# Sparse attention and a multiplicative FFN on one core: batch 0 loaded first, a weight fold hosted behind FFN products, and both score groups in one phase

## The chip, the cores and the metric

The kernel runs on one core of one Trainium2 chip. The metric is the device time of one execution, in microseconds (us). A time is given as the median of several executions with their range. The span of a profile runs from the first to the last recorded instruction; it was about 1.7 us shorter than the device time. Executions of this kernel on one core are also marked fast or slow: slow is one that was over 1.5% above the fastest of the same kernel. Comparisons use the fast ones.

## The reference

Attention over 8 batches, 8 heads, 576 positions and 64 channels; half of the heads see the last 32 positions ("local"), half see every 32nd position ("strided"). Its output is the input of a feed-forward network (FFN) in which two projections are multiplied.

```python
rel = pos[:, None] - pos[None, :]
mask_local = (rel >= 0) & (rel < 32)                       # heads 0..3
mask_strided = (rel >= 0) & (pos[None] % 32 == pos[:, None] % 32)   # heads 4..7
attn = softmax(where(mask, q @ k.T / 8, -1e9))
x = (attn @ v).transpose(0, 2, 1, 3).reshape(4608, 512)
h = ((x @ w1) * (x @ w2)) @ w3                             # w1, w2: 512x1024; w3: 1024x1024
return h @ w_out                                           # w_out: 1024x512
```

No activation stands between `w3` and `w_out`, so the kernel computes their product once ("the fold", `w34 = w3 @ w_out`) and each FFN tile of 512 tokens needs only `x @ w1`, `x @ w2`, the product, and `@ w34`.

## The kernel before

Everything is cast to fp16 on load. A "pair" is two heads of one batch, so a batch has four pairs, two local and two strided. Five staging buffers (`stgp`) hold what has been loaded and not yet been cast. The attention of a pair is a list of phases; the function `host` interleaves phases with "units", the halves of FFN products, so that TensorE always has a product to do while the other engines work on the attention.

```python
def load_w3(pr):                    # 1 MB; staging buffer -> two w3n tiles (a pool of 2)
    st = stgp.tile([P, 2, DF], FP32, tag="stg"); nc.sync.dma_start(st, ...)
    ...                             # one cast on DVE, one on ACT
def load_local(b):                  # q, k: 96 partitions; casts on GpSimd, 0.87 us each
    ...
    st = stgp.tile([P, 4, LT, D], FP32, tag="stg")       # v with 32 earlier rows per block
    nc.sync.dma_start(st[:, :, 0, :], v[b, 0:4, 0:P]...)
    for h in range(4):
        nc.sync.dma_start(st[:, h, 1:LT, :], _ap(v[b, h], (LQ - 32) * D, ...))
    nc.gpsimd.tensor_copy(out=vt[:, :, :, 0:D], in_=st)
def load_strided(b): ...            # q, k, v: 72 partitions, casts on GpSimd

def ph_T(s, which):                 # transpose q or k of a pair, copy to SBUF
    ps = psM.tile([P, 1024], FP16, tag="m")              # psM: ONE buffer in PSUM
    ...
    if which == "q": nc.scalar.copy(out=o, in_=i)
    else:
        nc.vector.tensor_copy(out=o, in_=i)
        nc.gpsimd.memset(t[:, S:640], 0.0)
def ph_S(s, g):                     # scores of half a pair (64-row products), exp, mask
    ...
    nc.scalar.activation(out=pte[0:kr], in_=sps[0:kr, :, 0:288], func=AF.Exp, ...)
    nc.vector.tensor_mul(ptm[...], pte[...], <mask>)     # two inputs in SBUF
    nc.gpsimd.memset(ptm[:, 576:640], 0.0)
def ph_PV(s, g): ...                # probabilities x values, reciprocal, scaling
def ph_T2(s): ...                   # transpose the result into xT, through psM too

for p in range(np_):                # the order of the phases
    stream.append(lambda s=s: ph_S(s, 0))
    if p + 1 < np_: stream.append(lambda s=pairs[p + 1]: ph_T(s, "q"))
    stream.append(lambda s=s: ph_S(s, 1))
    if p >= 1: stream.append(lambda s=pairs[p - 1]: ph_T2(s))
    stream.append(lambda s=s: ph_PV(s, 0))
    if p + 1 < np_: stream.append(lambda s=pairs[p + 1]: ph_T(s, "k"))
    stream.append(lambda s=s: ph_PV(s, 1))

load_wo(); load_w3(0); load_w3(1)
... fold of blocks 0..3 ...         # 8 transposes and 8 products each
load_local(0); load_w3(2); load_w3(3); load_strided(0); load_w12()
host(later, 14)                     # fold of blocks 4..7 among batch 0's attention
load_local(1); att_only(batch_end[0]); load_strided(1)
for tch in range(NTILE):            # FFN tile tch, with the attention of batch tch + 1
    ...
```

The softmax here doesn't subtract the row's maximum and nothing guards it: scores larger than these inputs give would overflow.

## Time and profile before

| before | |
|---|---|
| time, median of 3 (range) | 312.8 us (312.19 to 313.06) |
| span of the profiled execution | 311.9 us |
| first FFN product starts | 65.4 us |
| a stage (one FFN tile and one batch of attention), tiles 1 to 5 | 28.71 us, within 0.02 |
| last stage (FFN tile alone) | 20.96 us |

A "stage" in this text is the distance between the first FFN products of two consecutive tiles, by the start times of the matmuls.

The page of the profile: busy time of two engines, and, in 40 slices of the span, the busy tenths of TensorE (PE), its granted clock and the share of the DMA engines.

```profile
span 311.9 us, 6533 instructions
...
PE 277.8 (89%) x2561; PEld 144.2 (46%) x2561; DVE 188.9 (61%) x361; ACT 134.6 (43%) x221; POOL 100.3 (32%) x192
...
PE   0285757689999999999999999999999999999994
...
PEclk9999897569999999999999999999999999999999
DMA  6999999998769989999895868660002001102003
```

PE is full from the ninth slice, near 66 us. Before it DMA is full. The table of stretches shows the same with numbers (busy us of each engine in the stretch, then granted clock, DMA share and GB/s):

```profile
core 0: us, PE busy (x) PEld busy (x) DVE busy (x) ACT busy (x) POOL busy (x), PEclk, DMA share, GB/s
8.00:16.00 8.00, 2.42 (x12) 1.34 (x13) 2.33 (x5) 2.68 (x3) 0.00 (x0) 1.00 1.05 363
40.00:48.00 8.00, 5.35 (x58) 3.14 (x58) 6.30 (x11) 4.18 (x8) 1.92 (x4) 0.97 1.05 364
...
56.00:64.00 8.00, 4.85 (x72) 3.96 (x72) 6.72 (x13) 2.69 (x5) 3.36 (x9) 0.50 0.92 191
64.00:72.00 8.00, 7.63 (x62) 3.93 (x60) 4.77 (x11) 3.97 (x7) 5.17 (x8) 0.75 0.96 201
100.00:140.00 40.00, 39.74 (x410) 20.80 (x409) 29.05 (x57) 20.83 (x35) 17.75 (x31) 1.00 0.97 209
```

From 8 to 72 us the DMA engines are busy all the time, and TensorE is not: 2.42 of 8 us at first, and 4.85 of 8 us at half clock just before the FFN starts. From 100 us on PE has 39.74 of 40 us. So two different limits hold, loads before about 65 us and TensorE after it.

Two further readings prepare the change. In the chain of work that ended last, the four products after a score phase (L224) take 0.97 us instead of 0.86:

```profile
77.12 0.86 PE bps L303 x4
77.98 0.24 PE sps L224 x8
78.22 0.97 PE aps L294 x4
79.19 0.26 PE ps L201 x8
```

The start times of the single products say where the 0.11 us comes from: leaving the 64-row score products costs about 95 ns (127 ns instead of 32), and ahead of them entering costs another 95 ns (310 ns instead of 215). The Trainium skill ("TensorEngine Tiling (Array Packing)", Key Properties) says that a change of the tiling mode drains TensorE; it gives no time for it. And in the stages from 123 to 267 us PE waited for almost nothing (waited-for instruction, us in total, times, longest):

```profile
engine line waited for: us in total, times, longest us
PE aps L294 <- ACT xT_112 L273: 1.3, 5, 0.3
```

### The profile page before, as it was taken

To read this page: it belongs to the slowest core of one execution; us is meant where nothing else is said; L and a number is where in the kernel's file an instruction comes from. 1 tells how busy PE (TensorE), PEld (TensorE's weight loads), DVE (VectorE), ACT (ScalarE), POOL (GpSimd) and SP (SyncE) were. 2 spreads that over 40 slices of the span, in tenths; PEclk is the share of its full clock that TensorE was granted. 3 is DMA by queue.
4 is the path that set the end of the run, shared out by engine and by line. 5 is a ranking of instruction groups with operands and counts; after the bars stand their busy time and mean duration, and the time that the engine had idled before them with its cause. 6 is when DMAs were issued, how large, how long until landed. Compare 5 with 4: busy or idle time off the path is not lost.

```text
span 311.9 us, 6533 instructions
## 1 busy us (share of the span) xinstructions
PE 277.8 (89%) x2561; PEld 144.2 (46%) x2561; DVE 188.9 (61%) x361; ACT 134.6 (43%) x221; POOL 100.3 (32%) x192
## 2 busy tenths in 40 slices
PE   0285757689999999999999999999999999999994
PEld 0133334554554554555455554555554555444441
DVE  1234378868767676777678566778765666442421
ACT  2323435345545544544454455445544543332330
POOL 5041520557463364435356171733230000000000
PEclk9999897569999999999999999999999999999999
DMA  6999999998769989999895868660002001102003
GB/s 227 371 228 324 229 376 232 177 210 150 183 165 261 196 189 248 226 182 206 243 223 113 217 191 159 143 187 36 0 36 101 2 3 74 62 0 101 35 2 136
DMA packets 48287, 50.23 MB, mean 161 GB/s; under 512 B 26496, under 2 KB 32640, under 8 KB 48256
## 3 DMA queue, kind: packets, MB, share of 16 engines
q1 hardware_dynamic: 48256, 49.82, 63.1%
q8 instruction: 20, 0.33, 0.5%
q14 instruction: 11, 0.09, 0.1%
HBM read 40.37 MB, written 9.44 MB: 160 GB/s over the span
## 4 chain that ended last, share of the span: by engine, by line
PE 83%; DVE 6%; ACT 5%; DMA 3%; issue 1%; SPq 0%; DVEq 0%; ACTq 0%
PE ops L317 26%; PE bps L303 20%; PE aps L294 20%; PE ps L201 5%; PE sps L224 5%; PE xps L250 4%; DMA st<-in_moe_w_dram 3%; PE ps L266 3%; ACT pte L229 2%; DVE w_115 L350 1%; ACT xT_112 L273 1%; DVE w3T_117 L346 1%; DVE xqs L258 1%; PE ps L344 1%; DVE t L212 1%
## 5 line engine op out<-in xcount | busy, mean ns | idle before, releaser
L297 ACT COPY asb<-aps 128x512 f32<-128x512 f32 x72 | 42.2, 586 | 68.8 <-PE aps L294 51.3
L229 ACT ACTIVATE pte<-sps 128x576 f16<-128x576 f32 (+1 forms) x64 | 41.6, 650 | 36.7 <-PE sps L224 36.1
L173 POOL CAST t<-st 72x1024 f16<-72x1024 f32 x32 | 33.0, 1059 | 25.0 <-DMA st<-in_q_dram 15.1
L258 DVE TENSOR_TENSOR xqs<-xps,rcp 96x384 f16<-96x384 f32 (+1 forms) x64 | 39.6, 619 | 2.1
L154 POOL CAST t<-st 96x768 f16<-96x768 f32 x32 | 26.9, 867 | 29.2 <-DMA st<-in_q_dram 17.1
L303 PEld LDWEIGHTS <-w2h 128*128 128x128 f16 x288 | 24.5, 98 | 22.1 <-issue 1.3
L294 PEld LDWEIGHTS <-w1h 128*128 128x128 f16 x288 | 24.6, 99 | 21.9 <-issue 0.6
L201 PEld LDWEIGHTS <-t 72*128 72x128 f16 (+1 forms) x448 | 25.1, 101 | 17.0 <-issue 4.0
L201 PE MATMUL ps<-id_79,t 72*128 72x72 f16 (+1 forms) x448 | 28.5, 206 | 3.1 <-ACT w3T_118 L347 2.8
L250 PEld LDWEIGHTS <-ptm 72*128 72x128 f16 (+1 forms) x448 | 23.2, 101 | 17.2 <-issue 2.2
L236 DVE TENSOR_TENSOR ptm<-pte,maskS 72x576 f16<-72x576 f16 x32 | 19.3, 603 | 17.7 <-ACT pte L229 17.5
L294 PE MATMUL aps<-xT_112,w1h 128*128 128x512 f16 x72 | 27.5, 382 | 1.6 <-ACT xT_112 L273 1.5
L232 DVE TENSOR_TENSOR ptm<-pte,maskL 128x576 f16<-128x576 f16 x32 | 18.4, 576 | 16.2 <-ACT pte L229 15.6
L294 PE MATMUL aps<-xT_109,w1h 128*128 128x512 f16 x72 | 27.8, 386 | 0.0
L303 PE MATMUL bps<-xT_109,w2h 128*128 128x512 f16 x72 | 27.6, 384 | 0.0
L294 PE MATMUL aps<-xT_111,w1h 128*128 128x512 f16 x72 | 27.5, 382 | 0.0
L294 PE MATMUL aps<-xT_110,w1h 128*128 128x512 f16 x72 | 27.5, 382 | 0.0
L303 PE MATMUL bps<-xT_110,w2h 128*128 128x512 f16 x72 | 27.3, 379 | 0.0
L303 PE MATMUL bps<-xT_112,w2h 128*128 128x512 f16 x72 | 27.3, 379 | 0.0
L303 PE MATMUL bps<-xT_111,w2h 128*128 128x512 f16 x72 | 27.2, 378 | 0.0
L329 ACT COPY osb<-ops 128x512 f32<-128x512 f32 x18 | 10.5, 586 | 33.0 <-PE ops L317 33.0
L224 PEld LDWEIGHTS <-t 64*128 64x128 f16 x448 | 11.1, 97 | 29.1 <-issue 22.5
(89 smaller groups left out, 415.0 us busy)
## 6 DMA issues: line engine op xcount, KB each, us to landing
st<-in_q_dram SPq DMA_DIRECT2D x16, 576.0 KB
st<-in_k_dram SPq DMA_DIRECT2D x16, 576.0 KB
out_dram<-osb SPq DMA_DIRECT2D x36, 256.0 KB
st<-in_moe_w_dram SPq DMA_DIRECT2D x8, 1024.0 KB
st<-in_v_dram SPq DMA_DIRECT2D x32, 160.0 KB
st<-in_v_dram SPq DMA_DIRECT2D x8, 576.0 KB
st<-in_moe_w_out_dram SPq DMA_DIRECT2D x2, 1024.0 KB
st<-in_v_dram SPq DMA_DIRECT2D x8, 128.0 KB
```

The source lines that it names most:

```text
L154: nc.gpsimd.tensor_copy(out=t[:, hp], in_=stv[:, 2 * hp:2 * hp + 2].rearrange("p h c d -> p c h d"))
L173: nc.gpsimd.tensor_copy(out=t[:, hp], in_=stv[:, 2 * hp:2 * hp + 2].rearrange("p h c d -> p c h d"))
L201: pe(nc.tensor.transpose(ps[:, c * w:(c + 1) * w], src[:, c].rearrange("p h d -> p (h d)"), id16[0:w, 0:w]))
L224: pe(nc.tensor.matmul(sps[:, h, i * w:(i + 1) * w], s.tT["k"][r, ks:ks + P], s.tT["q"][r, w * t:w * t + w], start=True, stop=True))
L229: nc.scalar.activation(out=pte[0:kr], in_=sps[0:kr, :, 0:288], func=AF.Exp, bias=0.0, scale=scale)
L236: nc.vector.tensor_mul(ptm[0:kr, 0:576].rearrange("p (a x) -> p a x", x=w), pte[0:kr].rearrange("p h (a x) -> p (h a) x", x=w), _ap(maskS, ...
L250: pe(nc.tensor.matmul(xps[:, h, i * 65:(i + 1) * 65], ptm[0:kr, c0:c0 + P], vt[0:kr, 2 * (s.hp % 2) + h, g * m + i, :], start=True, stop=T ...
L258: nc.vector.tensor_mul(xqs[0:w, 0:m].rearrange("p i h d -> p h i d"), xv[:, :, :, 0:D], _ap(rcp, 0, [[rp, w], [4, 2], [1, m], [0, D]]))
L294: pe(nc.tensor.matmul(aps, w1h[:, ci, bass.ds(jc * P, P)], xT[ci][:, tok], start=(ci == 0), stop=(ci == KM - 1)))
L297: nc.scalar.copy(out=asb, in_=aps)
L303: pe(nc.tensor.matmul(bps, w2h[:, ci, bass.ds(jc * P, P)], xT[ci][:, tok], start=(ci == 0), stop=(ci == KM - 1)))
L317: pe(nc.tensor.matmul(st["ps"], lhs(ci), rhs(ci), start=(ci == 0), stop=(ci == KF - 1)))
```

## The change

Its intent is to start the FFN earlier and to shorten the stages. Batch 0 and `w1`, `w2` are loaded first; `w_out` and `w3` come behind them and the fold moves from the start to the second FFN tile. Both score phases of a pair become one, so TensorE enters and leaves the 64-row products once per pair. The 32 earlier rows of each value block are copied on chip from the block before, where they were loaded twice. Probabilities and transposed keys live in fixed tiles whose zero padding is written once, which removes 96 small GpSimd memsets. The 72-partition loads are split into 64 and 8.

```diff
+    kTL = [consts.tile([P, 32 + S], FP16, name=f"kTL{i}") for i in range(2)]
+    kTS = [consts.tile([P, S + 56], FP16, name=f"kTS{i}") for i in range(2)]
+    ptms = [consts.tile([P, 640], FP16, name=f"ptm{i}") for i in range(4)]
... (zero padding written once, on DVE)
-        nc.sync.dma_start(st[:, :, 0, :], v[b, 0:4, 0:P].rearrange("h p d -> p h d"))
         for h in range(4):
-            nc.sync.dma_start(st[:, h, 1:LT, :],
-                              _ap(v[b, h], (LQ - 32) * D, [[D, P], [LQ * D, LT - 1], [1, D]]))
+            nc.sync.dma_start(st[32:P, h], v[b, h].rearrange("(t p) d -> p t d", p=LQ))
         vt = v16L[b % 2]
-        nc.gpsimd.tensor_copy(out=vt[:, :, :, 0:D], in_=st)
+        for pr in (bass.ds(32, 32), bass.ds(64, 64)):
+            nc.gpsimd.tensor_copy(out=vt[pr, :, :, 0:D], in_=st[pr])
+        nc.vector.tensor_copy(out=vt[0:32, :, 1:LT, 0:D], in_=vt[96:P, :, 0:LT - 1, 0:D])
+    def load72(st, src):
+        nc.sync.dma_start(st[0:64], sv[0:64])
+        nc.sync.dma_start(st[64:SQ], sv[64:SQ])
... (ph_T, ph_S: fixed tiles, memsets gone, one local mask for all blocks)
+    add(lambda: ph_T(pairs[1], "q"))
     for p in range(np_):
         s = pairs[p]
-        stream.append(lambda s=s: ph_S(s, 0))
-        if p + 1 < np_:
-            stream.append(lambda s=pairs[p + 1]: ph_T(s, "q"))
-        stream.append(lambda s=s: ph_S(s, 1))
+        add(lambda s=s: ph_S(s, 0), lambda s=s: ph_S(s, 1))
         if p >= 1:
-            stream.append(lambda s=pairs[p - 1]: ph_T2(s))
+            add(lambda s=pairs[p - 1]: ph_T2(s))
-        stream.append(lambda s=s: ph_PV(s, 0))
-        if p + 1 < np_:
-            stream.append(lambda s=pairs[p + 1]: ph_T(s, "k"))
-        stream.append(lambda s=s: ph_PV(s, 1))
+        add(lambda s=s: ph_PV(s, 0))
+        add(lambda s=s: ph_PV(s, 1))
+        if p + 1 < np_:
+            add(lambda s=pairs[p + 1]: ph_T(s, "k"))
+        if p + 2 < np_:
+            add(lambda s=pairs[p + 2]: ph_T(s, "q"))
... (start)
-    load_wo(); load_w3(0..1); fold 0..3; load_local(0); load_w3(2..3); load_strided(0); load_w12()
-    host(fold 4..7, 14); load_local(1); att_only(batch_end[0]); load_strided(1)
-    for tch in range(NTILE):
+    load_local(0); load_strided(0); load_w12(); load_local(1); load_strided(1)
+    load_wo(); load_w3(0..3)
+    host([lambda: None], batch_end[0])
+    load_local(2)
+    host(ab_halves(0), batch_end[1])
+    load_strided(2)
+    load_local(3)
+    host(ab_halves(1) + fold, batch_end[2] - 6)
+    load_strided(3)
+    host(o_halves(0) + o_halves(1), batch_end[2])
+    for tch in range(2, NTILE):
```

(The last part is condensed: calls on one line, and loops written as ranges.)

More of the change, by code (lines that the diff above doesn't have):

```diff
@@ L65 @@
     make_identity(nc, id16)
-    maskL = consts.tile([P, LT, LQ], FP16)
+    maskL = consts.tile([P, LQ], FP16)
     nc.gpsimd.memset(maskL, 1.0)
-    nc.gpsimd.affine_select(out=maskL[:, 0, :], in_=maskL[:, 0, :], compare_op=ALU.is_ge,
-                            fill=0.0, base=0, pattern=[[1, LQ]], channel_multiplier=-1)
-    nc.gpsimd.affine_select(out=maskL[:, 0, :], in_=maskL[:, 0, :], compare_op=ALU.is_ge,
-                            fill=0.0, base=31, pattern=[[-1, LQ]], channel_multiplier=1)
-    nc.gpsimd.affine_select(out=maskL[:, 1:LT, :], in_=maskL[:, 1:LT, :], compare_op=ALU.is_ge,
-                            fill=0.0, base=32, pattern=[[0, LT - 1], [1, LQ]], channel_multiplier=-1)
-    nc.gpsimd.affine_select(out=maskL[:, 1:LT, :], in_=maskL[:, 1:LT, :], compare_op=ALU.is_ge,
-                            fill=0.0, base=-1, pattern=[[0, LT - 1], [-1, LQ]], channel_multiplier=1)
+    nc.gpsimd.affine_select(out=maskL, in_=maskL, compare_op=ALU.is_ge,
+                            fill=0.0, base=32, pattern=[[1, LQ]], channel_multiplier=-1)
+    nc.gpsimd.affine_select(out=maskL, in_=maskL, compare_op=ALU.is_ge,
+                            fill=0.0, base=-1, pattern=[[-1, LQ]], channel_multiplier=1)
     sel = consts.tile([4, 18, 4], FP16)
@@ L96 @@
     v16S = [consts.tile([SQ, 4, ST, D + 1], FP16, name=f"v16S{i}") for i in range(2)]
+    kTL = [consts.tile([P, 32 + S], FP16, name=f"kTL{i}") for i in range(2)]
+    kTS = [consts.tile([P, S + 56], FP16, name=f"kTS{i}") for i in range(2)]
+    ptms = [consts.tile([P, 640], FP16, name=f"ptm{i}") for i in range(4)]
     for i in range(2):
+        nc.vector.memset(kTL[i][:, 0:32], 0.0)
+        nc.vector.memset(kTS[i][:, S:S + 56], 0.0)
         nc.vector.memset(v16L[i][:, :, :, D], 1.0)
+        nc.vector.memset(v16L[i][0:32, :, 0, :], 0.0)
         nc.vector.memset(v16S[i][:, :, :, D], 1.0)
+    for i in range(4):
+        nc.vector.memset(ptms[i][:, 576:640], 0.0)
     xT = [consts.tile([P, NTOK], FP16, name=f"xT{cc}") for cc in range(4)]
@@ L158, in load_local @@
         st = stgp.tile([P, 4, LT, D], FP32, tag="stg")
-        nc.sync.dma_start(st[:, :, 0, :], v[b, 0:4, 0:P].rearrange("h p d -> p h d"))
         for h in range(4):
-            nc.sync.dma_start(st[:, h, 1:LT, :],
-                              _ap(v[b, h], (LQ - 32) * D, [[D, P], [LQ * D, LT - 1], [1, D]]))
+            nc.sync.dma_start(st[32:P, h], v[b, h].rearrange("(t p) d -> p t d", p=LQ))
         vt = v16L[b % 2]
-        nc.gpsimd.tensor_copy(out=vt[:, :, :, 0:D], in_=st)
+        for pr in (bass.ds(32, 32), bass.ds(64, 64)):
+            nc.gpsimd.tensor_copy(out=vt[pr, :, :, 0:D], in_=st[pr])
+        nc.vector.tensor_copy(out=vt[0:32, :, 1:LT, 0:D], in_=vt[96:P, :, 0:LT - 1, 0:D])
+    def load72(st, src):
+        sv = src.rearrange("h (p c) d -> p h (c d)", c=ST)
+        nc.sync.dma_start(st[0:64], sv[0:64])
+        nc.sync.dma_start(st[64:SQ], sv[64:SQ])
     def load_strided(b):
@@ L168, in load_strided @@
             st = stgp.tile([SQ, 4, ST * D], FP32, tag="stg")
-            nc.sync.dma_start(st, ten[b, 4:8].rearrange("h (p c) d -> p h (c d)", c=ST))
+            load72(st, ten[b, 4:8])
             t = qkp.tile([SQ, 2, ST, 2, D], FP16, tag=nm + "S")
@@ L177, in load_strided @@
         st = stgp.tile([SQ, 4, ST * D], FP32, tag="stg")
-        nc.sync.dma_start(st, v[b, 4:8].rearrange("h (p c) d -> p h (c d)", c=ST))
+        load72(st, v[b, 4:8])
         vt = v16S[b % 2]
@@ L202, in ph_T @@
                                    src[:, c].rearrange("p h d -> p (h d)"), id16[0:w, 0:w]))
-        t = att.tile([P, 640], FP16, tag=which + "T")
+        if which == "q":
+            t = att.tile([P, S], FP16, tag="qT", bufs=3)
+            tv = t
+        else:
+            t = (kTL if s.local else kTS)[s.hp % 2]
+            tv = t[:, 32:32 + S] if s.local else t[:, 0:S]
         s.tT[which] = t
         if s.local:
-            o, i = t[:, 0:S].rearrange("x (p c) -> x p c", c=n), ps[:, 0:S].rearrange("x (c p) -> x p c", p=w)
+            o, i = tv.rearrange("x (p c) -> x p c", c=n), ps[:, 0:S].rearrange("x (c p) -> x p c", p=w)
         else:
-            o, i = t[:, 0:S], ps[:, 0:S]
+            o, i = tv, ps[:, 0:S]
         if which == "q":
@@ L212, in ph_T @@
             nc.vector.tensor_copy(out=o, in_=i)
-            nc.gpsimd.memset(t[:, S:640], 0.0)
     def ph_S(s, g):
@@ L220, in ph_S @@
             t = g * m + i
-            ks = max(0, w * t - 32) if s.local else w * t
+            ks = w * t
             for h in range(2):
@@ L226, in ph_S @@
         pte = att.tile([P, 2, 288], FP16, tag="pte")
-        ptm = att.tile([P, 640], FP16, tag="ptm", bufs=3)
+        ptm = ptms[(2 * s.hp + g) % 4]
         s.ptm[g] = ptm
@@ L231, in ph_S @@
             pit = maskL.ap[0][0]
-            nc.vector.tensor_mul(ptm[:, 0:576].rearrange("p (h x) -> p h x", h=2), pte,
-                                 _ap(maskL, g * 288, [[pit, P], [0, 2], [1, 288]]))
+            nc.vector.tensor_mul(ptm[:, 0:576].rearrange("p (a x) -> p a x", x=w),
+                                 pte.rearrange("p h (a x) -> p (h a) x", x=w),
+                                 _ap(maskL, 0, [[pit, P], [0, 6], [1, w]]))
         else:
@@ L238, in ph_S @@
                                  _ap(maskS, 0, [[pit, kr], [0, 8], [1, w]]))
-        nc.gpsimd.memset(ptm[:, 576:640], 0.0)
     def ph_PV(s, g):
@@ L357, with add @@
     batch_end = {}
-    stream += [lambda: ph_T(pairs[0], "q"), lambda: ph_T(pairs[0], "k")]
+    def add(*fs):
+        stream.append(lambda: [f() for f in fs])
+    add(lambda: ph_T(pairs[0], "q"))
+    add(lambda: ph_T(pairs[0], "k"))
+    add(lambda: ph_T(pairs[1], "q"))
     for p in range(np_):
         s = pairs[p]
-        stream.append(lambda s=s: ph_S(s, 0))
-        if p + 1 < np_:
-            stream.append(lambda s=pairs[p + 1]: ph_T(s, "q"))
-        stream.append(lambda s=s: ph_S(s, 1))
+        add(lambda s=s: ph_S(s, 0), lambda s=s: ph_S(s, 1))
         if p >= 1:
-            stream.append(lambda s=pairs[p - 1]: ph_T2(s))
+            add(lambda s=pairs[p - 1]: ph_T2(s))
             if p % 4 == 0:
                 batch_end[p // 4 - 1] = len(stream)
-        stream.append(lambda s=s: ph_PV(s, 0))
+        add(lambda s=s: ph_PV(s, 0))
+        add(lambda s=s: ph_PV(s, 1))
         if p + 1 < np_:
-            stream.append(lambda s=pairs[p + 1]: ph_T(s, "k"))
-        stream.append(lambda s=s: ph_PV(s, 1))
-    stream.append(lambda: ph_T2(pairs[np_ - 1]))
+            add(lambda s=pairs[p + 1]: ph_T(s, "k"))
+        if p + 2 < np_:
+            add(lambda s=pairs[p + 2]: ph_T(s, "q"))
+    add(lambda: ph_T2(pairs[np_ - 1]))
     batch_end[B - 1] = len(stream)
@@ L385, in host @@
                 pos[0] += 1
-    def att_only(upto):
-        while pos[0] < upto:
-            stream[pos[0]]()
-            pos[0] += 1
-    load_wo()
-    for pr in range(2):
-        load_w3(pr)
-    fold = []
-    for jc in range(4):
-        for u in fold_halves(jc):
-            u()
     load_local(0)
-    for pr in range(2, 4):
-        load_w3(pr)
     load_strided(0)
     load_w12()
-    later = []
-    for jc in range(4, 8):
-        later += fold_halves(jc)
-    host(later, 14)
     load_local(1)
-    att_only(batch_end[0])
     load_strided(1)
-    for tch in range(NTILE):
+    load_wo()
+    for pr in range(4):
+        load_w3(pr)
+    host([lambda: None], batch_end[0])
+    load_local(2)
+    host(ab_halves(0), batch_end[1])
+    load_strided(2)
+    fold = []
+    for jc in range(KF):
+        fold += fold_halves(jc)
+    load_local(3)
[3 more added lines that the diff above has]
+    for tch in range(2, NTILE):
         units = ab_halves(tch) + o_halves(tch)
```

## The prediction

> **What bounds the kernel now.** From 65.4 us (the first FFN product) to the end TensorE is the limit: the table of stretches has PE busy 39.7 of 40 us at full clock, and stages with attention take 28.71 us, without it 20.98. Before 65.4 us it is loads: DMA share about 1.0 from 8 to 70 us, and the granted clock falls to 0.5 at 54 to 68 us.
>
> **Steady state.** Matmul start times show what joining the score groups is for: entering or leaving the 64-row score matmuls costs about 95 ns each (310 against 215 ns before them, 127 against 32 ns after the last). One phase per pair instead of two saves 8 x 95 = 0.75 us per batch, an estimated 5.2 us over batches 1 to 7. Removed POOL memsets (0.15 us each) are off the critical path. Against it: probabilities are now wanted only two FFN units (1.7 us) after the scores, and two transposes stand one unit apart with one PSUM buffer; 0 to 3 us of new waits.
>
> **Start.** PE work from the first FFN product on was 246.5 us; minus 0.9 (half clock) and 5.2, plus the fold now behind it (8 x (0.61 + 8 x 0.216) = 18.7 us), it is 259 us. Break-even: that product at 54 us, without later stalls.
>
> DMA costs from the profile: 96-partition loads of 0.59 MB 2.5 us; 72-partition ones 2.8 us (190 to 237 GB/s, against 387 for w1/w2, 410 for w3). The Trainium skill ("SBUF — State Buffer", Door 1: the DMA port swizzle) says partitions 0 to 63 reach only half the ports, about 218 GB/s; the trace agrees, so 64 + 8 instead of 72 gives little. The local v load is issue-bound[...], so 7.0 us. My queue estimate: batch 0 lands by 18 us, w1/w2 29, batch 1 46, w_out 51, w3 62, q and k of batch 2 67. First FFN product near 40 us.
>
> Then it stalls. DVE's order has the w_out and first w3 casts ahead of the first FFN products' evacuation: gated to about 50 and 55 us. w3's later tiles wait for the fold (two cast buffers) and hold three of five staging buffers, so batch 2's v is issued only after its q is cast: near 67 us, + 7 issue + 1 + 2.9 (two POOL casts of 1.47) + 0.6: its first value product near 76 to 79 us, PE idle 4 to 6 us before it. PE work left there is about 235 us, plus 3 us of fold waits (it ran 3.05 us per block alone, 2.34 of it PE) and 1 to 2 us of half clock: 315 to 319.
>
> **Prediction:** 316 us, 8 in 10 within 307 to 324. Faster by over 2%: 0.10; within: 0.55; slower: 0.35.
>
> **What would show it.** Right: first FFN product at 37 to 43 us; attention stages near 28.0 us; PE idle and DVE waiting on w_out between 42 and 55 us; a gap before batch 2's value products at 72 to 79 us, released by POOL's cast or the halo copy; DMA share still 1.0 until 75 us. Wrong: stages still 28.7; no gap near 75 us; w3 landed before 55 us.
>
> **What would make it wrong.** Loads overlapping better than the sum of their separate times (308 or less); waits between scores and values in every stage (over 322).

## The result, and the profile after

| | before | after |
|---|---|---|
| time, median (range) | 312.93 us (312.19 to 317.15) | 340.84 us (339.0 to 342.3) |
| ratio of fast runs | 1 | 1.0898, 95% interval 1.0827 to 1.0968 |
| first FFN product | 65.4 us | 43.6 us |
| first FFN product of the third tile | 123.7 us | 143.6 us |
| stages of tiles 2 to 6 | 28.70, 28.71, 28.71, 28.71, 27.45 | 30.09, 30.08, 29.84, 30.88, 27.20 |
| first FFN product of the third tile to the end | 188.2 us | 193.7 us |

One of the four executions of the kernel before, 317.15 us, is over 1.5% above its fastest, so it counts as slow and stays out of the ratio; the four of the kernel after are fast. Here and below a ratio is the mean time of one kernel's fast runs over the mean of the other's fast runs of the same rounds, so it isn't quite the ratio of the medians.

The change made the kernel 9% slower; 316 us had been predicted. The same parts of the page as before:

```profile
span 337.3 us, 6371 instructions
...
PE 279.1 (83%) x2561; PEld 148.1 (44%) x2561; DVE 195.7 (58%) x379; ACT 131.3 (39%) x221; POOL 100.4 (30%) x102
...
PE   1254487678975779998999899989889999999995
...
PEclk9999999959999999999999999999999999999999
DMA  8999999967636932696439656916801200201103
```

PE is busy for nearly the same time (279.1 us, 277.8 before), in a span that is 25 us longer: the difference is idle time. Digits of 5 to 8 now stand in slices that were full. Line numbers of the kernel after are 6 to 16 above those of before. The stretches (columns as before):

```profile
8.00:16.00 8.00, 1.89 (x24) 1.40 (x24) 1.77 (x3) 2.37 (x4) 5.58 (x6) 1.00 1.12 207
40.00:48.00 8.00, 6.03 (x53) 3.59 (x51) 5.62 (x9) 2.85 (x5) 6.53 (x6) 1.00 1.07 206
...
56.00:64.00 8.00, 6.96 (x89) 3.89 (x89) 7.25 (x15) 5.15 (x8) 0.00 (x0) 1.00 1.03 397
64.00:72.00 8.00, 3.15 (x15) 1.11 (x12) 1.33 (x4) 1.22 (x2) 3.14 (x4) 0.80 0.70 154
72.00:80.00 8.00, 7.78 (x90) 4.53 (x90) 5.12 (x10) 3.96 (x7) 4.33 (x4) 0.78 0.71 146
...
100.00:110.00 10.00, 6.44 (x73) 3.73 (x71) 4.73 (x10) 2.98 (x5) 2.72 (x3) 1.00 0.61 122
...
180.00:220.00 40.00, 37.21 (x388) 19.69 (x387) 28.99 (x54) 19.25 (x34) 16.11 (x14) 1.00 0.74 164
```

The start did what was wanted: between 56 and 64 us PE has 6.96 us of work at full clock where it had 4.85 at half clock. (The record of the granted clock begins at 51.66 us in this profile and at 16.87 us in that of the kernel before; for earlier stretches the column prints 1.00 without a record. FFN products at 46.7 to 48.0 us started 0.42 us apart, where 0.215 is full rate.) But from 64 to 72 us it has only 3.15 us, and in the stretch with the fold (100 to 110 us) 6.44 of 10. In the steady part, 180 to 220 us, it has 37.21 of 40 us where it had 39.49.

The hole at 64 us, in the chain of work that ended last (start, length, what):

```profile
57.29 0.95 ACT woh L123
...
58.26 10.46 DMA st<-in_q_dram
...
68.84 0.83 POOL t L160
...
69.72 0.66 PE ps L212 x6
70.39 1.71 PE bps L318 x4
```

The chain reads from top to bottom: ScalarE's cast of `w_out` frees a staging buffer at 58.24 us; only then is batch 2's query load issued, and it lands 10.46 us later. For the first 6 us of that the queue was still moving `w3`, which stood ahead of it, at 396 GB/s; the rest is its own transfer and that of the key. GpSimd casts it; the query transposes run; and the FFN products behind them take 1.71 us for four, twice the 0.86 us of the full clock (the record has the clock at 0.5 from 68.7 to 75.6 us). PE waited 4.9 us for that cast in one piece.

PE's largest waits from 64 to 145 us, which is the end of the first stage and the stage with the fold (waited-for instruction, us in total, times, longest):

```profile
PE ops L332 <- DVE w3T_133 L361: 4.9, 6, 1.7
PE ps L212 <- POOL t L160: 4.9, 1, 4.9
PE ps L212 <- ACT w3T_134 L362: 3.6, 2, 1.9
```

The fold's products wait 4.9 us in total for the copies of the transposed `w3` that they use, and the next transposes wait 3.6 us for the copy that frees the one PSUM buffer.

PE's waits in the steady stages, 143 to 292 us:

```profile
PE xps L265 <- DVE ptm_107 L252: 3.9, 4, 1.0
PE ps L212 <- DVE kTS_106 L228: 1.8, 4, 0.5
PE ps L212 <- DVE kTL_104 L228: 1.5, 2, 1.1
PE ps L212 <- DVE kTL_103 L228: 0.6, 2, 0.3
```

And one of the first kind from close up, in the timeline (start, us, engine, line, operation):

```profile
187.43 1.89 POOL L191 CAST v16S_102<-st 72x2048 f16<-72x2048 f32 x1
...
187.46 2.17 DVE L252 TENSOR_TENSOR ptm_107<-pte,maskS 72x576 f16<-72x576 f16 x1 [1.53 <-ACT pte L244]
...
188.34 0.38 PE L309 MATMUL aps<-xT_128,w1h 128*128 128x512 f16 x1
...
189.69 0.42 PE L265 MATMUL xps<-v16S_101,ptm_107 72*128 72x65 f16 x8 [0.97 <-DVE ptm_107 L252]
...
190.16 0.44 DVE L252 TENSOR_TENSOR ptm_108<-pte,maskS 72x576 f16<-72x576 f16 x1
```

GpSimd's cast of the next values (L191) starts at 187.43 us, DVE's mask product (L252) starts 0.03 us later and takes 2.17 us, until 0.3 us after the cast is over. The same operation on the other half takes 0.44 us at 190.16. The last FFN product starts at 188.34 us and the value product (L265), which had to wait for the mask product, at 189.69: 1.35 us between two starts, where two full-rate products stand 0.22 us apart. The Trainium skill ("SBUF — State Buffer", Who interferes with whom) says that a DVE instruction with two SBUF inputs contends with a GpSimd instruction that reads SBUF, and that one of the two is shut out for the whole instruction of the other. This trace agrees: mask products took 454 ns on the mean where no long GpSimd cast overlapped them and 1254 ns (at most 2171) where one did, whereas the scaling of the value products, whose large input is in PSUM, took 622 and 620 ns.

The same lock stands in the kernel before:

```profile
207.64 1.89 POOL L180 CAST v16S_104<-st 72x2048 f16<-72x2048 f32 x1 [4.92 <-DMA st<-in_v_dram]
...
208.35 2.34 DVE L232 TENSOR_TENSOR ptm<-pte,maskL 128x576 f16<-128x576 f16 x1 [1.18 <-ACT pte L229]
...
211.12 0.34 PE L250 MATMUL xps<-v16L_101,ptm 128*128 128x65 f16 x6
```

From 90 to 280 us, 20 of its 48 mask products overlap such a cast and take 756 ns on the mean, at most 2344. But the value product came late enough there: here at 211.12 us, with the mask product done at 210.69 and no wait of its own, and the stages are 28.71 us all the same. So the change did not bring the lock; it took away the distance that hid it.

### The profile page after: what moved, and what is told of

The parts are those of the page before. It is cut to its first block, busy times and chain, and to the rows that moved or that the text cites. A ratio compares the mean times of both kernels' runs of the same rounds, so it can differ in the third digit from the quotient of the medians.

```text
span 337.3 us, 6371 instructions
## 1 busy us (share of the span) xinstructions
PE 279.1 (83%) x2561; PEld 148.1 (44%) x2561; DVE 195.7 (58%) x379; ACT 131.3 (39%) x221; POOL 100.4 (30%) x102
## 4 chain that ended last, share of the span: by engine, by line
PE 53%; DVE 15%; DMA 12%; issue 11%; ACT 4%; POOL 4%; SPq 0%; POOLq 0%; DVEq 0%; ACTq 0%
PE ops L332 17%; PE bps L318 13%; PE aps L309 13%; DMA st<-in_q_dram 7%; PE ps L212 4%; DMA st<-in_v_dram 3%; DVE ptm_107 L252 3%; POOL t L160 2%; DMA st<-in_k_dram 2%; PE xps L265 2%; DVE xqs L273 2%; PE sps L239 2%; PE ps L281 2%; ACT pte L244 2%; DVE kTL_103 L228 1%
## 5 line engine op out<-in xcount | busy, mean ns | idle before, releaser
L312 ACT COPY asb<-aps 128x512 f32<-128x512 f32 x72 | 42.1, 585 | 80.1 <-PE aps L309 75.6
L212 PE MATMUL ps<-id_79,t 72*128 72x72 f16 (+1 forms) x448 | 30.3, 214 | 28.3 <-POOL t L160 16.9
L160 POOL CAST t<-st 96x768 f16<-96x768 f32 x32 | 25.9, 836 | 63.7 <-DMA st<-in_q_dram 35.4
L244 ACT ACTIVATE pte<-sps 128x576 f16<-128x576 f32 (+1 forms) x64 | 38.2, 648 | 11.8 <-PE sps L239 11.8
L226 ACT COPY t<-ps 128x576 f16<-128x576 f16 x32 | 20.5, 639 | 48.0 <-PE ps L212 47.7
L318 PEld LDWEIGHTS <-w2h 128*128 128x128 f16 x288 | 25.3, 99 | 27.4 <-issue 5.4
L318 PE MATMUL bps<-xT_125,w2h 128*128 128x512 f16 x72 | 28.2, 391 | 2.1 <-DVE abt_611 L320 2.1
L309 PE MATMUL aps<-xT_128,w1h 128*128 128x512 f16 x72 | 28.0, 389 | 1.1 <-ACT xT_128 L288 0.7
L309 PE MATMUL aps<-xT_125,w1h 128*128 128x512 f16 x72 | 28.2, 391 | 0.0
L309 PE MATMUL aps<-xT_127,w1h 128*128 128x512 f16 x72 | 28.0, 389 | 0.0
L309 PE MATMUL aps<-xT_126,w1h 128*128 128x512 f16 x72 | 28.0, 389 | 0.0
L318 PE MATMUL bps<-xT_128,w2h 128*128 128x512 f16 x72 | 27.8, 386 | 0.0
L318 PE MATMUL bps<-xT_127,w2h 128*128 128x512 f16 x72 | 27.8, 386 | 0.0
L318 PE MATMUL bps<-xT_126,w2h 128*128 128x512 f16 x72 | 27.7, 385 | 0.0
L346 DVE COPY osb<-ops 128x512 f32<-128x512 f32 x18 | 12.4, 688 | 14.8 <-PE ops L332 14.8
L271 DVE RECIPROCAL rcp<-xps 96x6 f32<-96x6 f32 (+1 forms) x64 | 12.2, 190 | 13.5 <-PE xps L265 13.4
L169 POOL CAST v16L_99<-st 32x1536 f16<-32x1536 f32 (+1 forms) x8 | 12.0, 1496 | 14.8 <-DMA st<-in_v_dram 14.5
```

Of the source, the lines that this page charges most:

```text
L160: nc.gpsimd.tensor_copy(out=t[:, hp], in_=stv[:, 2 * hp:2 * hp + 2].rearrange("p h c d -> p c h d"))
L212: pe(nc.tensor.transpose(ps[:, c * w:(c + 1) * w], src[:, c].rearrange("p h d -> p (h d)"), id16[0:w, 0:w]))
L271: nc.vector.reciprocal(out=rcp[0:w, :, 0:m], in_=xv[:, :, :, D])
L309: pe(nc.tensor.matmul(aps, w1h[:, ci, bass.ds(jc * P, P)], xT[ci][:, tok], start=(ci == 0), stop=(ci == KM - 1)))
L312: nc.scalar.copy(out=asb, in_=aps)
L318: pe(nc.tensor.matmul(bps, w2h[:, ci, bass.ds(jc * P, P)], xT[ci][:, tok], start=(ci == 0), stop=(ci == KM - 1)))
```

## The experiments

The theory had two parts, and the expectations use letters for what competed. **A**: the new order of the attention phases makes the waits in the stages. Its rivals put them on what else the change does in every batch, the halo copy, the fixed tiles and the split loads. Within A, **C** is the lock between GpSimd's casts and DVE's mask products, and **D** the shorter distances between phases, above all at the one PSUM buffer for transposes. The rest of the loss was looked for in the start: the fold on TensorE's time, and the order of the loads.

### e1: the kernel after, with the old order of phases

```diff
 # kernel after
-        add(lambda s=s: ph_S(s, 0), lambda s=s: ph_S(s, 1))
+        stream.append(lambda s=s: ph_S(s, 0))
+        stream.append(lambda s=pairs[p + 1]: ph_T(s, "q"))
+        stream.append(lambda s=s: ph_S(s, 1))
... (and ph_T(…, "k") between the two ph_PV again, query one pair ahead)
```

> The changed kernel with the attention order of the kernel before (two score phases per pair, transposes apart), nothing else undone. Theory A (the new order itself makes the waits of the steady stages): attention stages fall from 30.0-30.1 us to 28.6-28.8 us, total 332-335 us. Rival B (the waits come from the fixed key and probability tiles, the value halo copy or late loads): stages stay at 30 us, total 339-342 us.

Measured: 339.91 us (335.24 to 342.12; two of four slow), before 313.19; ratio of fast runs 1.0741 (1.0653 to 1.0829). The stages of tiles 2 to 5 are 28.87, 28.70, 28.71 and 28.70 us, as in the kernel before. The profiled execution was a slow one, so only one thing is read from it: even there a stage is no longer than in the kernel before. The fold's stage was 69.8 us, with half clock in parts of it, and the total missed what was expected. What follows: with the rest of the change in place, the old order takes the stage waits away. A holds.

### e2: the kernel before, with the new order of phases

```diff
 # kernel before
+        add(lambda s=s: ph_S(s, 0), lambda s=s: ph_S(s, 1))     # the whole order of after
-        t = att.tile([P, 640], FP16, tag=which + "T")
+        t = att.tile([P, 640], FP16, tag=which + "T", bufs=3 if which == "q" else 2)
-        ptm = att.tile([P, 640], FP16, tag="ptm", bufs=3)
+        ptm = att.tile([P, 640], FP16, tag="ptm", bufs=4)
```

> The kernel before with only the attention order of the change (both score groups in one phase, transposes next to each other). Theory A: stages of about 30.0 us instead of 28.7, total 320-323 us. Rival B: stages of 28.0 us, because only the switch cost of 0.75 us per batch is left as an effect, total 307-309 us.

Measured: 320.1 us (318.32 to 321.89), before 313.19; ratio 1.0197 (1.0126 to 1.0268). Stages 29.57 to 30.34 us but for the last with attention. So the new order alone costs 6 to 7 us, without the halo copy, the fixed tiles or the new start. In the profile 3.4 us of it are a later first FFN product (68.85 us instead of 65.44), and about 4 us come from longer stages. Together with e1 this settles A. It does not confirm C, since PE's waits from 99 to 274 us are others than in the kernel after:

```profile
PE xps L250 <- POOL ptm L239: 2.6, 3, 1.6
PE ps L201 <- DVE t L212: 1.9, 4, 0.6
PE xps L250 <- DVE ptm L236: 1.1, 3, 0.7
```

The longest is for the memset of the padding (L239), which the change had removed: it takes 0.14 us and stands in GpSimd's order behind casts of some 2 us.

### e3: both score groups joined, but with the old distances

```diff
 # kernel before; order per pair:
-  S0 | T q(p+1) | S1 | T2(p-1) | PV0 | T k(p+1) | PV1
+  S0 S1 | T q(p+1) | T2(p-1) | PV0 | T k(p+1) | PV1             # ptm: 4 buffers
```

> The kernel before with joined score groups, but the query transpose of the next pair and the output transpose put between scores and values, and the key transpose between the two value groups as before. Theory A1 (the distances make the waits, joining itself saves 0.75 us a batch): stages of 27.9-28.2 us, total 306-309 us. Rival A2 (joining itself makes the waits, two exponentials come at once to ScalarE): stages of 28.7 us or more, total 312 us or more.

Measured: 314.83 us (313.08 to 316.87), before 313.19; ratio 1.0047 (0.9998 to 1.0097). Most stages are 28.41 us, 0.3 less than before; 27.9 to 28.2, and 306 to 309 us in total, had been expected. The matmul starts show two gaps of 0.47 us per stage ahead of the output transposes, where 0.22 is normal: query and output transposes now stand one unit apart and share one PSUM buffer, which gives back some 0.5 of the 0.75 us. The FFN starts about 3 us later (68.6 us), so nothing is left in total. By this sum joining saves what the switch cost promised, and the shared buffer takes most of it back.

### e4: the kernel before, with the halo copy, fixed tiles and split loads

```diff
 # kernel before, with the parts of the change in load_local, load_strided, ph_T and ph_S;
 # start and order of phases as before
```

> The changed kernel with the start and the attention order of the kernel before: what is left of the change is the halo copies on chip, the fixed tiles without POOL memsets, and the 64 + 8 split loads. If these are neutral: 310-314 us, stages 28.7 us. If they carry part of the loss: 316 us or more. If the loads gain: first FFN product 1-3 us earlier than 65.4 us.

Measured: 318.51 us (316.91 to 319.59), before 313.19; ratio 1.0155 (1.0099 to 1.0211). Stages stay at 28.7 us; the first FFN product comes at 68.7 us, 3.3 us later, and the first stage is 31.28 us, 1.7 us longer. The last stage with attention is 28.69 us instead of 27.45. So these parts don't make the waits in the stages, but cost about 5 us, most of it at the start. The prediction had no term for that.

### e5: the kernel after without the fold (wrong result)

```diff
 # kernel after
     def fold_halves(jc):
-        ... 8 transposes, two copies, 8 products, cast
+        def copy_only(): nc.vector.tensor_copy(out=w34[:, jc, :], in_=woh[:, jc, :])
+        return [lambda: None, lambda: None, copy_only]
```

> The changed kernel without the fold's 64 transposes and 64 products and their evacuations (a plain copy of w_out stands for the folded weight, so the result is wrong on purpose); all loads and casts stay. Theory (the fold is fully exposed where the change puts it, with its waits): 27 to 30 us less than the changed kernel, so 311 to 314 us, against 18.7 us if only its TensorE work were exposed (322 us).

Measured: 316.02 us (315.33 to 317.5), before 313.74; ratio 1.0079 (1.0017 to 1.0142). 340.84 less 316.02 is 24.8 us, between the two values: 27 to 30 us had been expected, and 18.7 us, the fold's work on PE by the prediction's sum, was the rival. In the profile the third tile starts 20.4 us earlier; the rest falls in later stages. The first two stages take 36.61 and 43.06 us without it, 36.29 and 63.72 with it. The third tile starts at 123.2 us, where it started before the change too (123.7). So even without the fold nothing is left of the 22 us by which the first FFN product came earlier. The run has a flaw: the units of the fold stay in the stream as empty ones, so from 96.4 to 105.7 us the attention phases stand without an FFN product between them, and the record has the clock at 0.5 from 99.3 to 109.6 us. The 43.06 us contain these waits, which the experiment made itself.

### e6: the kernel before without the fold (wrong result)

The same edit in the kernel before.

> The kernel before with the same removal (wrong on purpose). Theory (there the fold runs while TensorE waits for loads anyway): at most 6 us less, 307 to 312 us. Rival (the fold is as costly at the start): 290 to 295 us.

Measured: 314.69 us (313.36 to 317.01), before 313.74; ratio 1.0055 (0.9975 to 1.0135). The fold costs nothing in the kernel before; 307 to 312 us had been expected. Without it PE has nothing to do in one whole stretch (columns as above):

```profile
48.00:56.00 8.00, 0.00 (x0) 0.00 (x0) 4.92 (x3) 1.24 (x2) 0.00 (x0) 1.00 1.00 230
```

and the chain of work that ended last shows what the first FFN product waits for:

```profile
42.70 13.40 DMA st<-in_q_dram
...
56.16 0.83 POOL t L154
...
57.03 0.67 PE ps L201 x6
...
63.66 1.71 PE aps L294 x4
```

Batch 1's query was issued at 42.7 us, behind GpSimd's work for batch 0, and landed 13.4 us later, at 56.1 us; then come its cast, its transposes and its attention, and the FFN can't start before 63.66 us. Without the fold, then, the loads decide the start. With it the chain from 30 to 65 us runs over work of PE and DVE instead, and the first product comes 2 us later, at 65.44 us: two limits that lie 2 us apart. (The clock in the stretch above isn't recorded; its record begins at 67.16 us here.)

### e7: the kernel after, with GpSimd's casts cut per head

```diff
 # kernel after
             for hp in range(2):
-                nc.gpsimd.tensor_copy(out=t[:, hp], in_=stv[:, 2 * hp:2 * hp + 2]...)
+                for h2 in range(2):
+                    nc.gpsimd.tensor_copy(out=t[:, hp, :, h2, :], in_=stv[:, 2 * hp + h2])
... (the value casts too: four of one head each)
```

> The changed kernel with every GpSimd cast of queries, keys and values cut into pieces per head, so that none runs longer than about 0.6 us; same work otherwise. Theory C (a mask product of two SBUF operands stands still until a running GpSimd cast ends: 2.17 us instead of 0.45 where it met the 1.89 us value cast): mask products with overlap fall from 1.25 us mean to 0.8 or less, stages from 30.0 to 28.6-29.3 us, total 334-337 us. Rival D (the short distance alone makes the waits): stages stay at 29.7-30.1 us, total 339-342 us.

Measured: 336.25 us (335.33 to 337.64), before 313.74; ratio 1.0722 (1.0652 to 1.0791). Mask products that overlap a cast now take 655 ns on the mean, at most 816 (1254 and 2171 before the cut). PE's waits in the steady stages, to be held against the four lines of the kernel after:

```profile
PE ps L213 <- DVE kTL L229: 1.7, 3, 0.6
PE ps L213 <- POOL t L185: 1.6, 4, 0.4
```

The wait for the mask product is gone, and the stages of tiles 2 to 5 are 29.23, 29.22, 28.63 and 28.63 us, as C expected. That fits C and does not prove it alone, for e8 shortens them as much without touching the casts. What is left is D, the transposes that wait for the buffer that a DVE copy frees, and a new wait of 1.6 us for the casts themselves. The cut has its own price: GpSimd's busy time rose from 100.4 to 124.5 us for 136 more instructions, 0.18 us each.

### e8: the kernel after, with batch 2's local loads ahead of w3

```diff
 # kernel after
-    for pr in range(4): load_w3(pr)
     host([lambda: None], batch_end[0])
+    ab0 = ab_halves(0)
+    host(ab0[0:8], (pos[0] + batch_end[1]) // 2)
     load_local(2)
-    host(ab_halves(0), batch_end[1])
+    for pr in range(4): load_w3(pr)
+    host(ab0[8:], batch_end[1])
```

> The changed kernel with batch 2's local loads put in the queue ahead of w3 (behind w_out). Theory (TensorE's 5.2 us wait for batch 2's query at 64.5 us is the queue's order): that wait goes, second FFN tile starts at 73-76 us instead of 79.8, total 335-337 us. Rival (the sum of loads binds, the wait moves to w3): second tile at 74-80 us but a new wait before the fold, total 338-342 us.

Measured: 331.05 us (329.37 to 334.23), before 313.74; ratio 1.0564 (1.0474 to 1.0654). That is 9.8 us less than the kernel after, more than expected (335 to 337 us). The first stage falls from 36.29 to 29.02 us, because PE no longer waits for batch 2's query; the stage with the fold is still 64.88 us. The hole at 64 us is thus the place of that load in the queue, behind `w3`. In the profile 4.1 of the 9.8 us are gained by the start of the third tile. The rest comes later: the stages of tiles 2 to 5 are 28.53, 30.26, 28.20 and 28.40 us, although their order of phases and their casts are those of the kernel after. Only one value product waits for its mask product there (0.4 us), where four did. So in these runs the lock costs time only when a cast meets the mask product that TensorE needs next, and when the casts start depends on the loads.

### e9 and e13: can the good parts be had alone?

e13 is the kernel before with fixed tiles for keys and probabilities and without the 96 memsets; e9 is e13 with the order of e3 and the per-head casts of e7.

```diff
 # kernel before (e13)
-        t = att.tile([P, 640], FP16, tag=which + "T")           # keys
+        t = kTs[s.hp % 2]
-        ptm = att.tile([P, 640], FP16, tag="ptm", bufs=3)
+        ptm = ptms[(2 * s.hp + g) % 4]
-        nc.gpsimd.memset(ptm[:, 576:640], 0.0)                   # and that of t
```

> The kernel before with only the fixed key and probability tiles (zeroed once, no GpSimd memsets per use). Theory (they are neutral, the halo copies cost the 4 us): 312-315 us. Rival (the memsets had kept GpSimd's casts away from the mask products, or the fixed tiles make new waits): 316-319 us.

> The kernel before, its start unchanged, with joined score groups at the old distances, GpSimd casts cut per head, and fixed key and probability tiles (no GpSimd memsets). Theory (the joined phase saves 0.75 us a batch once neither distance nor a running GpSimd cast holds the mask product): all attention stages 27.9-28.3 us, none near 29.7, total 308-311 us. Rival (joining saves only 0.3 us a batch, as in the spaced run before): stages 28.4 us, total 312-315 us.

Measured: e13 314.25 us (312.31 to 315.7), before 313.77, ratio 1.0027 (0.9963 to 1.0091): neutral. e9 315.94 us (314.63 to 319.25), before 314.11, ratio 1.0076 (1.0015 to 1.0136): a miss, 308 to 311 us had been expected. e9's first stage is 30.0 us, the others with attention are 28.4 to 29.3 us, and its FFN starts at 67.3 us.

### e10 and e11: half of the first FFN tile ahead of batch 1's attention

If the FFN waits for batch 1's query, TensorE could do the first tile's products meanwhile. e11 does that to the kernel before, e10 to e9. Both also give half of the `w1` and `w2` casts to ScalarE.

```diff
 # kernel before (e11)
-            host(units[0:12], mid)
+            if tch == 0:
+                for u in units[0:8]: u()
+                host(units[8:12], mid)
+            else: host(units[0:12], mid)
... (batch 1's first transposes moved behind the end of batch 0; w1, w2 casts shared)
```

> The kernel before with only the placing ahead and the shared w1/w2 casts, split score phases as before. Theory: stages 28.7 us, first product at 54-61 us, total 306-311 us. Rival as above: 312 us or more.

> As the run above, and the first FFN tile's first half placed ahead of batch 1's transposes and scores, with half of each w1/w2 cast moved from VectorE to ScalarE; loads and fold stay as in the kernel before. Theory (in the kernel before the first FFN product waits for batch 1's query and key, landed at 56 us, though it needs neither): first product at 54-61 us instead of 65.4, total 302-308 us. Rival (VectorE's casts and batch 0's chain bind the start): first product at 62 us or later, total 308 us or more.

Measured: e11 318.75 us (316.53 to 322.4, one of four slow), before 314.11, ratio 1.0141 (1.0045 to 1.0237); e10 319.68 us (315.47 to 323.16, three of six slow), ratio 1.0104 (1.0031 to 1.0176). Both miss. In e11 the first FFN product comes at 60.71 us, 4.7 us earlier, and the stage after it takes 37.57 us instead of 29.57: the products done ahead are then missing between the phases of batch 1's attention, which fits the longer stage but was not tested apart. This would be the kernel after in small: an earlier first product isn't a gain if what it would have hidden then stands open.

### e12: old order for batch 0, joined and spaced from batch 1 on

```diff
 # kernel of e3
+        if p < 4:  S0 | T q(p+1) | S1 | ...      # as before
+        else:      S0 S1 | T q(p+1) | ...        # as e3
```

> The kernel before with its attention order kept for batch 0 and joined score groups at the old distances from batch 1 on; VectorE's order of the start is then the same as before. Theory (the spaced run lost at the start what its stages of 28.41 us gained): first product at 65-67 us, stages 28.4 us, total 309.5-312 us, some 0.5% under the kernel before. Rival: 313-315 us, the stages' gain is lost elsewhere.

Measured: 313.2 us (311.4 to 314.4), before 314.45; ratio 0.9967 (0.9922 to 1.0012). The late start of e3 is mostly mended (65.9 us), most later stages are 28.41 us, but the first is 30.6. In total 309.5 to 312 us had been expected. It is the best version and not clearly better than the kernel before.

### e14 and e15: what in e4 costs time?

e4's casts of `w1` and `w2` ended late (58.1 to 64.3 us; before 45.8 to 58.0). e14 is e4 with the 72-partition loads unsplit; e15 is e14 with per-head casts.

```diff
 # kernel of e4 (e14)
     def load72(st, src):
-        nc.sync.dma_start(st[0:64], sv[0:64])
-        nc.sync.dma_start(st[64:SQ], sv[64:SQ])
+        nc.sync.dma_start(st, sv)
```

> The run with the change's halo copies and fixed tiles on the start of the kernel before, but with the strided loads in one piece again. Theory (there the 64 + 8 split made VectorE's program put the four w1/w2 casts last, ending at 64.3 us instead of 58.0, which held batch 1's key load): casts end by 60 us, total 312-316 us against 318.5. Rival (the longer value casts on GpSimd and the halo copy cost it): total stays at 317-320 us.

> The run with halo copies and unsplit strided loads, with GpSimd's casts cut per head. Theory (the value cast in two instructions doubles the time that GpSimd runs beside VectorE, and stopped mask products carry the loss): 313-316 us against 318. Rival (the loss is elsewhere): 317-320 us.

Measured: e14 318.04 us (317.16 to 319.75), before 314.45, ratio 1.0117 (1.0063 to 1.0171); e15 322.33 us (320.55 to 322.98), before 313.77, ratio 1.0296 (1.0237 to 1.0354). In e14 those casts end at 48.8 to 60.1 us, much earlier than in e4, and the total hardly moves (312 to 316 us had been expected): late casts of `w1` and `w2` are not the cause. Its first product comes at 67.6 us and its first stage takes 31.7 us, each still 2.1 us more than in the kernel before. In e15 the casts that could hold DVE up are short, and the kernel is slower still (313 to 316 us had been expected), so the lock with GpSimd isn't shown to be the cause either. Fixed tiles alone are neutral (e13). What is left for the 3 to 4 us is the on-chip halo copy together with the key layout and the local mask that the change gave it: the halo copy has other loads, replaces one value cast on GpSimd of 1.47 us by two of about 1.5 us and adds a DVE copy of 0.50 us. No run takes these apart, and how they become 3 to 4 us stays open.

## Why the prediction was wrong

Put in a row, the ratios give a share to each part: 1.0155 for the halo copy, tiles and loads (e4), 1.0741 / 1.0155 = 1.0577 for the new start (e1 over e4), 1.0898 / 1.0741 = 1.0146 for the joined order on top of it. (Their product is 1.0898 by construction, as each is the quotient of two neighbours.) e1 and e4 were timed in the same rounds, the kernel after in others, and the intervals of 0.007 to 0.009 each way leave the last factor wide open, so these are shares and not exact parts. The new start costs the most.

**What was right.** The queue: batch 0 landed near 20 us (predicted 18), `w1` and `w2` near 30 (29), batch 1 at 49.2 (46), `w_out` at 52.2 (51), `w3` near 64 (62), q and k of batch 2 at 69 (67). The first FFN product came at 43.6 us, against "37 to 43 us". Half right was "DVE waiting on w_out": DVE had no wait for that load, but its cast of `w_out` stood ahead of the first FFN evacuation at 55.9 us, and PE waited 2.1 us for that. "DMA share still 1.0 until 75 us" did not come: it was 0.70 from 64 to 72 us. The fold on TensorE's time was put at 18.7 us and 3 us of waits, 21.7 together; without it the kernel is 24.8 us faster (e5, with the flaw named there). The split of the 72-partition loads gave no gain: the stretch from 12 to 20 us with them ran at 198 GB/s, and from 30 to 36 us the kernel before, unsplit, ran at 228. The Trainium skill ("DMA: Bandwidth & Descriptors", Why a DMA increments its semaphore by 16 and not by 1) says that a load is spread over the largest number of engines, at most 16, that divides the partitions on both sides, 12 for 72 and 16 for 64, which would be a reason for the split. It doesn't help here, in agreement with the port limit that the prediction quoted.

The budget was break-even "at 54 us, without later stalls", and the prediction took the stalls too small in three steps.

**First failed step: "0 to 3 us of new waits", "attention stages near 28.0 us".** Stages took 30.0 us. The five from tile 2 to tile 6 sum to 148.1 us; the prediction's 28.0 and a last one of 26.7 (27.45 less the 0.75 saved) give 138.7. The 9.4 us between are waits. Four value products come 1.35 us after the product before them where 0.22 is normal, 4.5 us in all (3.9 us in the table of waits, which counts the idle time alone); the transposes wait 5.0 us for copies out of the one transposition buffer. The mechanism is one that I had not looked for: a cast on GpSimd that reads SBUF stops the mask product for up to 2.17 us, and now TensorE stands at that mask product. The trace also shows what let such a cast go: the last query transposition of a batch, now two pairs ahead, ran at 184.97 us, the cast of the next batch's query, loaded long before, started at 185.46 after 6.5 us without work, and the value cast behind it met the mask product at 187.43. No run changed this one distance alone, so that origin is read from the trace and not tested. The prediction did name "waits between scores and values in every stage" as what would make it wrong, and they came; I had charged only for the shorter distance, at most 3 us, and not for a collision. e1 and e2 show that the order makes the waits. The split between the two kinds rests on the trace: in e7, with short casts, the stages of tiles 2 to 5 sum to 115.7 us instead of 120.9, but in e8, with the casts as they were and other loads ahead of them, to 115.4.

**Second failed step: "its first value product near 76 to 79 us".** It came at 83.3 us. The prediction looked at batch 2's values; PE stood still for its query, which the new order wants one pair earlier, from 64.9 to 69.7 us. That query's load waited for a staging buffer until 58.26 us and then, for some 6 of the 10.46 us until it landed, behind `w3`. Then came products at half rate. The values themselves were cast by 78.0 us and their halo copied by 81.0. About 6 us late; e8 shows that the load's place is the cause: there the wait is gone and the first value product of batch 2 comes at 78.0 us. The issue term was wrong as well: "+ 7 issue" came from the kernel before, where four issues of the values took 7.8 us, and from a rate per row that the prediction drew from it. The traces don't bear a rate out: in the kernel after the same four issues took 5.69 us at 1.77 us, behind the loads of batch 0's query and key, and 1.96 us at 70.46 us, when the queue was nearly empty (DMA share 0.13 from 69 to 70 us).

**Third failed step: "PE work left there is about 235 us, plus 3 us of fold waits … and 1 to 2 us of half clock".** After the first value product of batch 2 it took 254.0 us, some 14 us more. 9.4 of it are the stages of the first step. The rest, about 5 us, lies in the stage with the fold, where PE waited 4.9 + 3.6 = 8.5 us for the fold's copies instead of 3.

The excess is then 6 + 9.4 + 5, about 20 us. The prediction's sum, made of profile times, was 315 to 319 us, and the span was 337.3.

**A term that was missing.** The halo copy, with its key layout and mask, was taken for neutral. e4 and e14 put it and the fixed tiles at 3 to 5 us in the kernel before, most of it at the start, and e13 finds the fixed tiles alone neutral. No run isolates it in the kernel after, so it isn't a further term of the sum above: whatever it costs there lies inside the steps already named.

**Where the 22 us of head start went.** Before, the first two stages took 58.3 us; after, 100.0 us, 41.7 more. PE was busy for 58.0 of them before and for 81.3 after. So 18.4 us are added idle time: batch 2's query (4.9), the first FFN evacuation (2.1), the fold's copies (8.5) and smaller waits. 18.7 us are the fold's own work, by the prediction's sum. The rest, some 5 us, fits the products at half rate until 51.7 us and from 68.7 to 75.6 us, but was not worked out product by product. In the kernel before the fold was free (e6), because it ran while TensorE was waiting for loads anyway. The bytes had to be loaded in either order; the change moved TensorE's free work out of the stretch that is limited by loads and put it into the one that TensorE limits.

## What to carry to other kernels

The fold's work on TensorE was free while everything waited for loads (e6); moved to where TensorE is the limit, it cost its length and the waits between its steps, so an earlier first product is a gain only if the loads and buffers behind it keep up. Before reordering phases, follow what each one frees: here, as the trace reads, an earlier transposition freed a buffer and with it the casts that had waited for it, and one of them stopped the DVE product that TensorE needed next. Measure a switch cost before removing it, as here (0.75 us per batch), but keep the distances between dependent phases, or the waits will be larger than what was saved.

## What the Trainium skill lacked or had wrong

- "TensorEngine Tiling (Array Packing)", Key Properties: that a change of mode drains TensorE has no time beside it. Here going from full-height to 64-row products and back took about 95 ns each way (310 instead of 215 ns, 127 instead of 32 ns).
- "GPSIMD Engine Reference", section 3.1, Reconciling with measured numbers: in that table the dispatch has a time for DVE and none for GpSimd. Cutting casts per head cost 24.1 us of GpSimd's busy time for 136 more instructions, 0.18 us each (an estimate, since spans on GpSimd are rough, and the shapes changed too).
- "TensorE: Matmul & The Clock Gate", Part 1, warns that clock events in a trace can't be fully trusted, without an example. Here is one of a record that lacks its beginning: the kernel after has no clock record before 51.66 us, and the views print 1.00 for that time, while at 46.7 to 48.0 us FFN products started 0.42 us apart where 0.215 is full rate.
- No page that I read gives a figure for how far a full queue stretches the issue of a load: the same four issues took 5.69 us behind other loads and 1.96 us on a nearly empty queue (kernel after, at 1.77 and 70.46 us).
